# Softmax denominators of two heads in one product, and the extra MLP columns in one matmul per term

## The chip, the core and the metric

The kernel runs on one core of a Trainium2 chip. The metric is the device time of one launch in microseconds (us). Runs of one kernel on this core mostly agree within 0.3%. A run that is over 1.5% above the fastest of its kernel counts as slow and is left out of the ratios. The profile is of one execution; its "span" is some 1.8 us shorter than the device time. The engines are PE (matmul; PEld is its weight load), DVE (vector), ACT (scalar), POOL, and SP, which issues the transfers. The granted clock is the share of full speed at which the profile shows PE running.

## The reference

For four tokens of width 576: a layer norm, then the sum of three things.

```python
def reference(A_x, A_k_cache, A_v_cache, A_wq, A_wo, B_x, B_w1, B_w2, B_w3, B_w4):
    xn = _layernorm(A_x)
    return A_x + _A_ref(xn, ...) + _B_ref(xn, ...)
# _A_ref: 32 query heads on 16 K/V heads of 128, one query per token, softmax over
#         the last 2048 keys of the cache, then @ wo
#     scores = einsum(q, k) * Dh**-0.5;  p = softmax(scores);  o = einsum(p, v);  o @ wo
# _B_ref: a mixer (whose shifted part is zero for one token) and an MLP with 4608 columns
#     x1 + gelu(layernorm(x1) @ w3) @ w4
```

The K and V windows are 67 MB of bf16, the weights wq, wo, w3 and w4 another 20 MB. All of it is read once.

## The kernel before

Each of the 16 K/V heads is loaded as one K tile and one V tile of 2.1 MB, from a pool of six such tiles. The heads pass through a software pipeline with one "turn" per head. In turn t, head t gets its scores, head t-1 its softmax, head t-2 its product with V, head t-3 its output scaling and transposes. The parts that the change touches:

```python
    def sm_exp(h):
        E[h] = ptp.tile([P, SC, QD], BF16, tag="e", name="E", bufs=1)
        rs = small.tile([P, 1], F32, tag="rs", bufs=3)
        nc.scalar.activation(out=E[h][:]..., in_=S_ps.pop(h)[:], func=ACT.Exp, scale=scale, accum_out=rs[:])
        st["rs", h] = rs
    def sm_den(h):       # sums the denominators over the partitions of one query, on PE
        dn = ps_m.tile([P, 1], F32, tag="m", name="dn")
        nc.tensor.matmul(out=dn[:], lhsT=same_j[:], rhs=st.pop(("rs", h))[:], start=True, stop=True)
        st["dn", h] = dn
    def sm_rec(h):
        rd = small.tile([P, 1], F32, tag="rd", bufs=4)
        nc.vector.reciprocal(out=rd[:], in_=st.pop(("dn", h))[:])
        st["rd", h] = rd
    def o_scale(h):
        O_sb[h] = bigp.tile([P, NSL, Dh], F32, tag="big", name="O_sb")
        nc.scalar.activation(out=O_sb[h][:], in_=O_ps.pop(h)[:], func=ACT.Copy, scale=st.pop(("rd", h))[:, 0:1])
    ...
    for t in range(Hkv):
        hm, hv, hf, hp = t - 1, t - 2, t - 3, t - 4
        for s in range(NSL):
            ...
            if s == 0:
                if hm >= 0: sm_max(hm)
                if hv >= 0: sm_rec(hv)
                ...
                if hf >= 0: o_scale(hf)
                k_transpose(t, 1)
```

In turn 7 the MLP's first product (w3) is done in three rounds. In the third, 128 columns that w4 needs in another order are multiplied as three strided matmuls per term; DVE moves the transposed results on:

```python
    if e and r == 2:
        for lo, rhs in x_cols(w3[:, base + m:base + F // 2]):     # 16, 12 and 100 columns, permuted
            ...
            mms.append((row[:, lo:hi, 1].rearrange(...), rhs))
    ...
    nc.vector.tensor_copy(out=xs[0:NX, NFM:, :], in_=gT_all[0:NX, n * m:, 0:B])
    nc.vector.tensor_copy(out=xs[:, NFM - 1, :], in_=gT_ps[:, 0, 1, 0:B])
```

## Time and profile before

| kernel before | value |
|---|---|
| device time, median of 6 runs | 211.56 us (211.21 to 211.69) |
| PE, DVE, ACT busy | 149.7, 114.4, 34.1 us of 209.6 |
| transfer queue, share of 16 DMA engines' span | 97.6% |
| bytes read | 87.17 MB, about 430 GB/s in the steady slices |
| start of PE's last 12 products / end of the span | 205.9 / 209.6 us |

Busy time is a sum over a whole run, so 71% of PE does not say whether PE is ever waited for. The transfers' row of the slices does (the page cuts the span into 40 slices and gives for each the busy share in tenths).

### The profile page before, as it was taken

To read this page: it belongs to the slowest core of one execution; us is meant where nothing else is said; L and a number is where in the kernel's file an instruction comes from. 1 tells how busy PE (TensorE), PEld (TensorE's weight loads), DVE (VectorE), ACT (ScalarE), POOL (GpSimd) and SP (SyncE) were. 2 spreads that over 40 slices of the span, in tenths; PEclk is the share of its full clock that TensorE was granted. 3 is DMA by queue.
4 is the path that set the end of the run, shared out by engine and by line. 5 is a ranking of instruction groups with operands and counts; after the bars stand their busy time and mean duration, and the time that the engine had idled before them with its cause. 6 is when DMAs were issued, how large, how long until landed. Compare 5 with 4: busy or idle time off the path is not lost.

```text
span 209.6 us, 2422 instructions
## 1 busy us (share of the span) xinstructions
PE 149.7 (71%) x984; PEld 60.1 (29%) x998; DVE 114.4 (55%) x167; ACT 34.1 (16%) x64; POOL 9.0 (4%) x32
## 2 busy tenths in 40 slices
PE   0357297599690039668999989659895956898794
PEld 0123132233130013223444333213331312343452
DVE  3611877895910083926507898465949391764100
ACT  7612201021020001111120312110111111113100
POOL 4610000000000000000000300000000000000000
PEclk9999589999787559788999999997998796999679
DMA  7999999999999999999999999999999999999992
GB/s 301 400 419 431 428 435 428 431 427 422 470 401 424 438 425 425 437 435 428 435 431 428 428 415 445 425 438 419 433 441 422 421 439 438 423 424 450 421 399 84
DMA packets 6703, 87.33 MB, mean 417 GB/s; under 512 B 758, under 2 KB 1034, under 8 KB 1700
## 3 DMA queue, kind: packets, MB, share of 16 engines
q1 hardware_dynamic: 6684, 87.17, 97.6%
q8 instruction: 8, 0.13, 0.2%
q10 hardware_dynamic: 8, 0.00, 0.0%
q14 instruction: 3, 0.02, 0.0%
HBM read 87.17 MB, written 0.00 MB: 416 GB/s over the span
## 4 chain that ended last, share of the span: by engine, by line
DMA 66%; DVE 15%; PE 13%; issue 2%; ACT 1%; SPq 1%; POOL 1%; DVEq 0%; POOLq 0%; ACTq 0%
DMA kn<-in_A_k_cache_dram 42%; DVE kt L253 12%; DMA vn<-in_A_v_cache_dram 10%; DMA w_sb<-in_B_w_dram 7%; DMA wq_sb<-in_A_wq_dram 6%; PE S L366 4%; PE g_ps L495 3%; PE q_ps L310 2%; PE oT L431 1%; PE O L418 1%; PE acc L212 1%; DVE PT L400 1%; DVE mx L372 1%; PE S L388 1%; DVE qz L342 1%
## 5 line engine op out<-in xcount | busy, mean ns | idle before, releaser
L366 PE MATMUL S<-kt,qz 128*128 128x512 bf16 x242 | 73.7, 427 | 33.9 <-DVE kt L253 31.9
L253 DVE STREAM_TRANSPOSE kt<-kn 128x2048 int32<-128x2048 int32 x32 | 73.4, 2296 | 26.1 <-DMA kn<-in_A_k_cache_dram 24.7
L366 PEld LDWEIGHTS <-qz 128*128 128x128 bf16 x256 | 23.9, 107 | 62.9 <-issue 45.8
L418 PE MATMUL O<-vn,PT 128*32 128x512 bf16 x256 | 23.4, 406 | 8.0 <-DMA vn<-in_A_v_cache_dram 8.0
L394 ACT ACTIVATE E<-S 128x512 bf16<-128x512 f32 x16 | 9.5, 597 | 96.6 <-PE S L388 96.6
L400 DVE STREAM_TRANSPOSE PT<-E 128x512 bf16<-128x512 bf16 x16 | 11.4, 710 | 13.9 <-ACT E L394 13.9
L425 ACT ACTIVATE O_sb<-O,rd 128x512 f32<-128x512 f32 x16 | 11.0, 687 | 37.2 <-PE O L418 37.2
L441 DVE TENSOR_REDUCE on<-oT 128x8 bf16<-128x128 f32 x16 | 4.6, 290 | 19.8 <-PE oT L431 19.8
L418 PEld LDWEIGHTS <-PT 128*32 128x32 bf16 x256 | 5.8, 94 | 29.4 <-issue 29.1
L431 PE MATMUL oT<-ident_w,O_sb 128*128 128x128 f32 x64 | 12.6, 333 | 0.3 <-ACT O_sb L425 0.3
L372 DVE TENSOR_REDUCE mx<-S 128x1 f32<-128x512 f32 x16 | 10.5, 658 | 1.2 <-PE S L366 1.1
L431 PEld LDWEIGHTS oT<-ident_w,O_sb 128*128 128x128 f32 x64 | 8.2, 164 | 5.3 <-issue 4.3
L388 PE MATMUL S<-nm,j_row 8*128 8x512 bf16 x16 | 6.5, 404 | 1.9 <-DVE nm L384 1.7
L404 PE MATMUL dn<-rs,same_j 128*128 128x1 f32 x32 | 6.2, 264 | 0.4 <-DVE g_x L523 0.4
L404 PEld LDWEIGHTS dn<-rs,same_j 128*128 128x128 f32 x32 | 5.0, 195 | 4.4 <-issue 3.7
L495 PE MATMUL g_ps<-w_sb,ln2T 128*32 128x512 bf16 (+5 forms) x65 | 6.2, 406 | 0.0
L354 PE MATMUL S<-negbig,ohT 4*128 4x512 bf16 x16 | 6.2, 385 | 0.0
L310 PE MATMUL q_ps<-wq_sb,xnT 128*32 128x512 bf16 x40 | 4.2, 610 | 2.1 <-DMA wq_sb<-in_A_wq_dram 2.1
L212 PE MATMUL acc<-wo_sb,op 128*4 128x288 bf16 x64 | 5.5, 324 | 0.0
L212 PE MATMUL acc<-w_sb,gT 128*4 128x288 bf16 x70 | 5.1, 298 | 0.4 <-DMA w_sb<-in_B_w_dram 0.4
L523 DVE COPY g_x<-gT_ps 128x64 f32<-128x64 f32 (+1 forms) x3 | 0.6, 198 | 8.2 <-PE gT_ps L509 8.2
L527 POOL TENSOR_TENSOR g_u<-g_x 128x180 f32<-128x180 f32 x1 | 0.5, 487 | 103.1 <-DVE g_x L523 103.1
(92 smaller groups left out, 79.2 us busy)
## 6 DMA issues: line engine op xcount, KB each, us to landing
kn<-in_A_k_cache_dram SPq DMA_DIRECT2D x16, 2048.0 KB, 25.7
vn<-in_A_v_cache_dram SPq DMA_DIRECT2D x16, 2048.0 KB, 21.7
wo_sb<-in_A_wo_dram SPq DMA_DIRECT2D x4, 1152.0 KB, 37.5
w_sb<-in_B_w_dram SPq DMA_DIRECT2D x1, 4608.0 KB
wq_sb<-in_A_wq_dram SPq DMA_DIRECT2D x1, 4096.0 KB
w_sb<-in_B_w_dram SPq DMA_DIRECT2D x1, 2592.0 KB, 11.0
w_sb<-in_B_w_dram SPq DMA_DIRECT2D x2, 576.0 KB, 34.1
w_sb<-in_B_w_dram SPq DMA_DIRECT2D x1, 864.0 KB
```

Source lines behind the costliest of these rows:

```text
L212: nc.tensor.matmul(out=acc_of(i), lhsT=lhsT, rhs=rhs[:, i * CW:(i + 1) * CW], start=False, stop=False, skip_group_check=True)
L253: nc.vector.transpose(out=kt[:], in_=src)
L366: nc.tensor.matmul(out=S_ps[h][:], lhsT=qz[:, z0:z0 + P], rhs=kt[:, ib, c0:c0 + SC, e:2 * QD:2].rearrange("p c k -> p (c k)"), start=False ...
L372: nc.vector.reduce_max(out=mx[:], in_=S_ps[h][:], axis=AX.X)
L388: nc.tensor.matmul(out=S_ps[h][:], lhsT=j_row[:], rhs=st.pop(("nm", h))[:, 0:1].to_broadcast([NJ, NW]), start=False, stop=False, skip_grou ...
L394: nc.scalar.activation(out=E[h][:].rearrange("p c k -> p (c k)"), in_=S_ps.pop(h)[:], func=ACT.Exp, scale=scale, accum_out=rs[:])
L400: nc.vector.transpose(out=PT[h][:], in_=E.pop(h)[:])
L404: nc.tensor.matmul(out=dn[:], lhsT=same_j[:], rhs=st.pop(("rs", h))[:], start=True, stop=True)
L418: nc.tensor.matmul(out=O_ps[h][g * QD:(g + 1) * QD], lhsT=PT[h][:, c, :], rhs=vn[:, :, c, :], start=(s == 0), stop=False, skip_group_check ...
L425: nc.scalar.activation(out=O_sb[h][:], in_=O_ps.pop(h)[:], func=ACT.Copy, scale=st.pop(("rd", h))[:, 0:1])
L431: nc.tensor.transpose(out=oT[:, s, :], in_=o[:, s, :], identity=ident_w[:, s * NJ:s * NJ + P])
L495: nc.tensor.matmul(out=out, lhsT=ln2T[:, k, :], rhs=rhs, start=(j == 0), stop=False, skip_group_check=True)
```

## The change

It is meant to take instructions off PE and DVE. The row sums of two heads go into two columns of one tile, so one product and one reciprocal serve both. The 128 extra MLP columns are multiplied in their natural order by one matmul per term; ScalarE permutes them while it copies them out, and takes over three DVE copies, now in five pieces. The core of the diff:

```diff
     def sm_exp(h):
-        rs = small.tile([P, 1], F32, tag="rs", bufs=3)
+        if h % 2 == 0:
+            st["rs"] = small.tile([P, 2], F32, tag="rs", name="rs", bufs=3)
-                             accum_out=rs[:])
+                             accum_out=st["rs"][:, h % 2:h % 2 + 1])
     def sm_den(h):
+        if h % 2 == 0:
+            return
-        dn = ps_m.tile([P, 1], F32, tag="m", name="dn")
+        dn = ps_m.tile([P, 2], F32, tag="m", name="dn")
     def sm_rec(h):
+        if h % 2 == 0:
+            return
-        rd = small.tile([P, 1], F32, tag="rd", bufs=4)
+        rd = small.tile([P, 2], F32, tag="rd", bufs=4)
         nc.vector.reciprocal(out=rd[:], ...)
+        for k in range(2):
+            st["rd", h - 1 + k] = rd[:, k:k + 1]
     def mlp_g(r):
-                    for lo, rhs in x_cols(w3[:, base + m:base + F // 2]):
-                        ... mms.append((row[:, lo:hi, 1].rearrange(...), rhs))
+                    mms.append((row[:, :, 1], w3[:, base + m:base + F // 2]))
+        if r == 2:
+            for lo, src in x_cols(g_ps[QD:2 * QD, :, 1]):
+                ... nc.scalar.activation(out=g_x[QD:2 * QD, lo:hi]..., in_=src, func=ACT.Copy)
     def mlp_turn(r):
-            nc.vector.tensor_copy(...)      # three on DVE
+            nc.scalar.activation(...)       # five on ScalarE
```

More of the change, by code (lines that the diff above doesn't have):

```diff
@@ L392, in sm_exp @@
         E[h] = ptp.tile([P, SC, QD], BF16, tag="e", name="E", bufs=1)
-        rs = small.tile([P, 1], F32, tag="rs", bufs=3)
+        if h % 2 == 0:
+            st["rs"] = small.tile([P, 2], F32, tag="rs", name="rs", bufs=3)
         nc.scalar.activation(out=E[h][:].rearrange("p c k -> p (c k)"), in_=S_ps.pop(h)[:], func=ACT.Exp, scale=scale,
-                             accum_out=rs[:])
-        st["rs", h] = rs
+                             accum_out=st["rs"][:, h % 2:h % 2 + 1])
     def sm_turn(h):
@@ L402, in sm_den @@
     def sm_den(h):
-        dn = ps_m.tile([P, 1], F32, tag="m", name="dn")
-        nc.tensor.matmul(out=dn[:], lhsT=same_j[:], rhs=st.pop(("rs", h))[:], start=True, stop=True)
-        st["dn", h] = dn
-    def sm_rec(h):
-        rd = small.tile([P, 1], F32, tag="rd", bufs=4)
-        nc.vector.reciprocal(out=rd[:], in_=st.pop(("dn", h))[:])
-        st["rd", h] = rd
+        if h % 2 == 0:
+            return
+        dn = ps_m.tile([P, 2], F32, tag="m", name="dn")
+        nc.tensor.matmul(out=dn[:], lhsT=same_j[:], rhs=st.pop("rs")[:], start=True, stop=True)
+        st["dn"] = dn
+    def sm_rec(h):
+        if h % 2 == 0:
+            return
+        rd = small.tile([P, 2], F32, tag="rd", bufs=4)
+        nc.vector.reciprocal(out=rd[:], in_=st.pop("dn")[:])
+        for k in range(2):
+            st["rd", h - 1 + k] = rd[:, k:k + 1]
     def pv(h, s):
@@ L424, in o_scale @@
         O_sb[h] = bigp.tile([P, NSL, Dh], F32, tag="big", name="O_sb")
-        nc.scalar.activation(out=O_sb[h][:], in_=O_ps.pop(h)[:], func=ACT.Copy, scale=st.pop(("rd", h))[:, 0:1])
+        nc.scalar.activation(out=O_sb[h][:], in_=O_ps.pop(h)[:], func=ACT.Copy, scale=st.pop(("rd", h)))
     def o_turn(h):
@@ L473 @@
     g_sb = {}
+    g_x = const.tile([P, P], F32, name="g_xt")
     def mlp_g(r):
@@ L487, in mlp_g @@
                 if e and r == 2:
-                    for lo, rhs in x_cols(w3[:, base + m:base + F // 2]):
-                        sizes = rhs.shape[1:]
-                        hi = lo + sizes[0] * sizes[1] * (sizes[2] if len(sizes) > 2 else 1)
-                        names = "x y z"[:2 * len(sizes) - 1]
-                        kw = dict(zip(names.split()[1:], sizes[1:]))
-                        mms.append((row[:, lo:hi, 1].rearrange(f"p ({names}) -> p {names}", **kw), rhs))
+                    mms.append((row[:, :, 1], w3[:, base + m:base + F // 2]))
                 for out, rhs in mms:
@@ L499, in mlp_g @@
         nc.scalar.activation(out=g_sb[r][0:m], in_=g_ps[0:m], func=ACT.Copy)
+        if r == 2:
+            for lo, src in x_cols(g_ps[QD:2 * QD, :, 1]):
+                sizes = src.shape[1:]
+                hi = lo + sizes[0] * sizes[1] * (sizes[2] if len(sizes) > 2 else 1)
+                names = "x y z"[:2 * len(sizes) - 1]
+                kw = dict(zip(names.split()[1:], sizes[1:]))
+                nc.scalar.activation(out=g_x[QD:2 * QD, lo:hi].rearrange(f"p ({names}) -> p {names}", **kw),
+                                     in_=src, func=ACT.Copy)
     def mlp_turn(r):
@@ L515, in mlp_turn @@
             for s in range(XS):
-                off = 4 * s if s < XC else 16 if s == XC else 28 + NX * (s - XA)
-                nc.tensor.transpose(out=gT_all[0:NX, n * m + s, :], in_=gs[e1, off:off + NX, 1],
+                off, k = (4 * s, 4) if s < XC else (16, 12) if s == XC else (28 + NX * (s - XA), NX)
+                nc.tensor.transpose(out=gT_all[0:k, n * m + s, :], in_=g_x[e1, off:off + k],
                                     identity=ident_f[e1, e1])
-            nc.vector.tensor_copy(out=xs[0:NX, NFM:, :], in_=gT_all[0:NX, n * m:, 0:B])
-            nc.vector.tensor_copy(out=xs[:, NFM - 1, :], in_=gT_ps[:, 0, 1, 0:B])
-            dst = xs[:, 16:18, :].unsqueeze(2)
-            gT_ps = gT_ps[:, :, 0:1]
+            for lo, hi, k in ((XB, XC, 4), (XC, XA, 12), (XA, XS, NX)):
+                nc.scalar.activation(out=xs[0:k, NFM + lo:NFM + hi, :],
+                                     in_=gT_all[0:k, n * m + lo:n * m + hi, 0:B], func=ACT.Copy)
+            nc.scalar.activation(out=xs[:, NFM - 1, :], in_=gT_ps[:, 0, 1, 0:B], func=ACT.Copy)
+            nc.scalar.activation(out=xs[:, 16:18, :], in_=gT_ps[:, :, 0, 0:B], func=ACT.Copy)
+            return
         nc.vector.tensor_copy(out=dst, in_=gT_ps[:, :, :, 0:B])
```

## The prediction

> **What bounds the kernel now.** I read the page first (busy shares, the slices, the queues), then the chain of waits, then the queue's own issues against what had been moved, then the last 5 us of the timeline. The page of the kernel before, parts 1 to 4:
>
> ```profile
> PE 149.7 (71%) x984; PEld 60.1 (29%) x998; DVE 114.4 (55%) x167; ACT 34.1 (16%) x64; POOL 9.0 (4%) x32
> ...
> DMA  7999999999999999999999999999999999999992
> GB/s 301 400 419 431 428 435 428 431 427 422 470 401 424 438 425 425 437 435 428 435 431 428 428 415 445 425 438 419 433 441 422 421 439 438 423 424 450 421 399 84
> ...
> q1 hardware_dynamic: 6684, 87.17, 97.6%
> ...
> DMA 66%; DVE 15%; PE 13%; issue 2%; ACT 1%; SPq 1%; POOL 1%; DVEq 0%; POOLq 0%; ACTq 0%
> ```
>
> No compute engine is near full, while the transfer queue works 97.6% of all 16 engines' span; only the first and the last slice are below 9. The GB/s row is flat at about 430 from slice 4 to slice 37. 87.17 MB at 430 GB/s is 203 us of a 209.6 us span.
>
> The chain gives 28% to DVE and PE, which looks like time to be won. It is not: the chain follows what released each issue (a K transpose or a row maximum frees a buffer), but while it passes through DVE or PE the DMA row is still at 9. I added up the bytes issued by the sync engine and took off those moved by the GB/s row. Just before each K or V load the queue still held 5.5 MB or more (12.7 us of work at 430 GB/s) up to 168 us, 3.5 MB (8 us) before the last V load at 179.7, and 1.3 MB (3 us) before the six w4 pieces at 189.7. It never ran dry.
>
> The end, from the timeline of the last 5 us (start, duration, engine, line, operation, idle before):
>
> ```profile
> 204.78 0.78 PE L212 MATMUL acc<-w_sb,gT 128*4 128x288 bf16 x10
> ...
> 205.94 1.04 PE L212 MATMUL acc<-w_sb,gT 128*4 128x288 bf16 x12 [0.39 <-DMA w_sb<-in_B_w_dram]
> ...
> 207.02 0.45 DVE L670 CAST fin<-acc 4x288 bf16<-4x288 f32 x1 [7.47 <-PE acc L212]
> ```
>
> PE has caught up, waits 0.39 us for the last w4 piece, does 12 products, and the result is copied and stored. So the time is: last byte landed (205.9) plus 3.7 us. Only what makes the last byte land earlier, or lets PE be late by over 0.39 us there, can move it.
>
> **What the Trainium skill says.** "DMA: Bandwidth & Descriptors", Measured: a 16 MB load reaches 425 GB/s on a core whose pair is idle, and Where 436 GB/s comes from puts the ceiling of the ports at 435.2. The trace agrees: its steady slices hold 415 to 450, mean about 430. There is nothing left to gain in rate, so the bytes set the time, and the change moves no bytes. "ScalarE: Activation LUTs", What ACT_TABLE_LOAD costs: an ACTIVATE with immediates takes 186 ns + 0.833 ns per element of a partition. The trace: the 128x512 copy (L499) took 597 ns against 612 so worked out, the 64x256 one 377 against 399; close enough to size the new small copies.
>
> **The change part by part.** The rows concerned (line, engine, operation, count, busy us, mean ns), from the groups by form:
>
> ```profile
> L404 PE MATMUL dn<-rs,same_j 128*128 128x1 f32 x32 | 6.2, 264 | 0.4 <-DVE g_x L523 0.4
> L404 PEld LDWEIGHTS dn<-rs,same_j 128*128 128x128 f32 x32 | 5.0, 195 | 4.4 <-issue 3.7 <-ACT E L394 0.7
> L495 PE MATMUL g_ps<-w_sb,ln2T 128*32 128x128 bf16 x5 | 2.0, 406 | 0.0
> L495 PE MATMUL g_ps<-w_sb,ln2T 128*32 128x100 bf16 x5 | 1.6, 330 | 0.0
> L409 DVE RECIPROCAL rd<-dn 128x1 f32<-128x1 f32 x16 | 2.6, 161 | 0.0
> L495 PE MATMUL g_ps<-w_sb,ln2T 128*32 128x16 bf16 x5 | 1.0, 198 | 0.0
> L495 PE MATMUL g_ps<-w_sb,ln2T 128*32 128x12 bf16 x5 | 0.9, 173 | 0.0
> L519 DVE COPY g_x<-gT_ps 20x40 f32<-20x40 f32 x1 | 0.2, 186 | 0.0
> L523 DVE COPY g_x<-gT_ps 128x8 f32<-128x8 f32 x1 | 0.1, 144 | 0.0
> L520 DVE COPY g_x<-gT_ps 128x4 f32<-128x4 f32 x1 | 0.1, 140 | 0.0
> ```
>
> - Denominators: 16 products (each recorded as two matmuls, 32 in all) become 8 of two columns. Gone in records: 16 x 264 ns = 4.2 us of matmul, 16 x 195 ns = 3.1 us of weight load. These overlap; in the timeline the next product starts 0.25 us after the pair's first, so PE wins 8 x 0.25 = 2.0 us.
> - Reciprocals: 8 of 16 go, 8 x 161 ns = 1.3 us of DVE records; the chain counts only 0.07 us each where one lies on it, because the next transpose starts before its record ends. So 0.6 to 1.3 us.
> - MLP round 3: three products per term of 16, 12 and 100 columns become one of 128. PE has 10 products fewer; the 25 of that stretch took 2.43 us, 0.097 each, so 1.0 us.
> - ScalarE gains eight copies: 16, 12 and 100 elements, then 16, 4, 20, 4 and 8. By the formula above 199 + 196 + 269 + 199 + 189 + 203 + 189 + 193 = 1.6 us (estimate), on an engine that is 16% busy. DVE loses three copies, 186 + 140 + 144 ns = 0.5 us.
>
> Sum: PE 3.0 us less, DVE 1.1 to 1.8 us less, ACT 1.6 us more, POOL and DMA unchanged. Beside a transfer queue that is never empty, all of it lies in hidden time: 0 us of it on the path that sets the end.
>
> **What it moves.** The built order shows the pair's reciprocal at the head of each odd head's turn, just behind the row maximum. An even head's output scaling used a reciprocal made one turn earlier; now it waits for this one. Scaling started at 44.80 with a reciprocal at 46.04 to 46.20 in that turn: 1.4 us later; in the MLP turn 97.40 against 99.48: 2.1 us. Its consumer, the output transposes, started at 47.78 in that turn (102.51 in the other): a scaling from 46.25 with its 0.69 us ends at 46.94, 0.8 us ahead. So the late scaling is absorbed, seven times over. Head 14, in the tail: its reciprocal moves from 190.41 to 192.84, its scaling from 192.55 to about 193.05; PE takes its transposes only at 195.85, behind head 15's products, which wait for the last V at 194.67. Absorbed too.
>
> In the MLP turn the five late copies end some 0.2 to 0.6 us after the DVE ones did (114.58), so tanh and the scaling of head 5 behind it on ACT come that much later; PE waited 0.31 us for that scaling already. PE's 1.0 us won just before pays for some of it. The result gT is first used at 192.74.
>
> **Rivals.**
> - *Compute was the bound after all.* For it: 28% of the chain, and turns from 118 to 133 us where DVE works without a pause. If PE's whole 3.0 us came off, 208.6 us. Against: DMA share 1.00 and 428 to 433 GB/s in that very stretch.
> - *A new wait takes its place*: scaling behind the pair's reciprocal, or ACT's copies in the MLP turn, hold PE up. Even 0.5 us in each of eight turns would be 4 us of compute: against it the 0.8 us slack; and it would have to eat 12.7 us of queue first. If it did nonetheless, 212 to 215 us.
> - *The tail*: PE has only 0.39 us in hand before the last w4 piece. Were the last heads to finish 1 us later, the end would come 0.6 us later: 212.2 us. Against it: head 14's slack of over 2 us.
>
> **Range and chances.** The transfers set the time and don't change: 211.5 us. Three runs before lay between 211.21 and 211.69; I allow as much again for another chip and for a little of the second and third rivals: 210.7 to 212.3. A change of 2% is 4.2 us, more than all that PE and DVE win together on the path (so faster is 0.01), and slower by as much needs a dry queue (0.02).
>
> **What would show it.** Right: DMA row at 9 throughout, queue share near 97.6%, last w4 piece landing near 205.9 with a wait of PE on it; PE busy down by some 5 us of records, 16 matmuls of L404 fewer, 10 of the MLP fewer, ACT up by about 1.6 us; even heads' scaling waiting on the reciprocal instead of on the product. Wrong: a slice of the DMA row below 9 in the middle, a transfer wait between issue and an empty queue, or PE with no wait before its last 12 products.

## More of the kernel before

One more view of the kernel before is needed later: what ACT's output scaling waits for. These are rows of ACT's timeline (start us, duration us, engine, line, operation; in brackets the idle time before it and what ended it):

```profile
44.80 0.69 ACT L425 ACTIVATE O_sb<-O,rd 128x512 f32<-128x512 f32 x1 [2.45 <-PE O L418]
52.06 0.69 ACT L425 ACTIVATE O_sb<-O,rd 128x512 f32<-128x512 f32 x1 [2.45 <-PE O L418]
62.40 0.69 ACT L425 ACTIVATE O_sb<-O,rd 128x512 f32<-128x512 f32 x1 [2.45 <-PE O L418]
```

Every one of them starts when the product with V is done; the reciprocal is there already.

## The result, and the profile after

| | before | after |
|---|---|---|
| device time, median of 6 runs | 211.56 us | 211.38 us |
| lowest, highest | 211.21, 211.69 | 211.25, 211.52 |
| ratio after/before | | 0.9994 (0.9981 to 1.0007) |
| span of the profiled run | 209.6 us | 209.6 us |

A ratio here is the mean time of one kernel's fast runs over the mean of the other's in the same rounds, so it is not quite the ratio of the medians. The change has no measurable effect.

The page of the changed kernel, in the same order as the lines that the prediction shows of before:

```profile
PE 150.2 (72%) x958; PEld 58.2 (28%) x972; DVE 113.4 (54%) x156; ACT 34.8 (17%) x72; POOL 9.0 (4%) x32
...
DMA  7999999999999999999999999999999999999992
...
q1 hardware_dynamic: 6684, 87.17, 97.7%
...
DMA 66%; DVE 15%; PE 14%; ACT 1%; issue 1%; SPq 1%; DVEq 0%; ACTq 0%
```

The transfers' row is the same to the digit, the queue's share is 97.7% against 97.6%. PE has 26 matmuls fewer (984 to 958), yet its busy time rose by 0.5 us. That is the clock: the mean granted clock of this run was 0.868 against 0.885, and the score products that the change does not touch took 437 ns each instead of 427 (464 at 0.816 in the profile of run 7, 400 at 0.969 in that of run 9). PE's busy time is no measure of a change of this size; the count is.

The groups that the change touched, by form (line, engine, operation, count, busy us, mean ns, then idle before):

```profile
L406 PE MATMUL dn<-rs,same_j 128*128 128x2 f32 x16 | 3.5, 287 | 0.0
L413 DVE RECIPROCAL rd<-dn 128x2 f32<-128x2 f32 x8 | 1.3, 163 | 0.0
L507 ACT ACTIVATE g_xt<-g_ps 32x100 f32<-32x100 f32 x1 | 0.2, 233 | 0.0
L529 ACT ACTIVATE g_x<-gT_ps 20x20 f32<-20x20 f32 x1 | 0.2, 159 | 0.0
```

Two columns cost little more than one did (287 and 163 ns against 264 and 161), so nearly half of that work is gone. ACT's eight copies took 146 to 233 ns each, 1.3 us in all; its busy time rose by only 0.7 us because they overlap.

The output scaling on ACT, for the same three heads as shown of before:

```profile
46.19 0.69 ACT L430 ACTIVATE O_sb<-O,rd 128x512 f32<-128x512 f32 x1 [3.94 <-DVE rd L413]
51.71 0.69 ACT L430 ACTIVATE O_sb<-O,rd 128x512 f32<-128x512 f32 x1 [2.16 <-PE O L423]
77.63 0.69 ACT L430 ACTIVATE O_sb<-O,rd 128x512 f32<-128x512 f32 x1 [17.49 <-DVE rd L413]
```

Even heads (first and third row) now wait for the pair's reciprocal. The first is 1.4 us late, as worked out. The third is 15 us late, which was not worked out: in that turn the reciprocal stands on DVE behind a row maximum that waits for a K tile still being transferred. PE pays neither: over the whole run its output transposes waited 0.3 us for the scaling, before and after.

The end of the span:

```profile
205.92 1.01 PE L212 MATMUL acc<-w_sb,gT 128*4 128x288 bf16 x12 [0.61 <-DMA w_sb<-in_B_w_dram]
...
206.64 0.29 PE L212 MATMUL acc<-w_sb,gT 128*4 128x288 bf16 x2
...
206.96 0.45 DVE L681 CAST fin<-acc 4x288 bf16<-4x288 f32 x1 [8.11 <-PE acc L212]
```

PE's last visible wait ends at 205.92 us, before it was 205.94. PE comes to it earlier by 0.2 us and waits 0.61 instead of 0.39 us. (The second row is a part of the first: the last two of the 12 products. They start at 206.64; run 12 shows why that matters.) Further up, after the MLP turn, the changed kernel issues its K loads about 1 us earlier (116.81 against 117.76, 131.31 against 132.36). By 167.94 (167.99 before) nothing is left of it: the next K and V come when the queue delivers them.

### The profile page after: what moved, and what is told of

Same layout as the page of the kernel before. It is cut to its first block, busy times and chain, and to the rows that moved or that the text cites. A ratio compares the mean times of both kernels' runs of the same rounds, so it can differ in the third digit from the quotient of the medians.

```text
span 209.6 us, 2356 instructions
## 1 busy us (share of the span) xinstructions
PE 150.2 (72%) x958; PEld 58.2 (28%) x972; DVE 113.4 (54%) x156; ACT 34.8 (17%) x72; POOL 9.0 (4%) x32
## 3 DMA queue, kind: packets, MB, share of 16 engines
q1 hardware_dynamic: 6684, 87.17, 97.7%
## 4 chain that ended last, share of the span: by engine, by line
DMA 66%; DVE 15%; PE 14%; ACT 1%; issue 1%; SPq 1%; DVEq 0%; ACTq 0%
DMA kn<-in_A_k_cache_dram 43%; DVE kt L253 12%; DMA vn<-in_A_v_cache_dram 10%; DMA w_sb<-in_B_w_dram 7%; DMA wq_sb<-in_A_wq_dram 6%; PE S L366 5%; PE g_ps L496 2%; PE q_ps L310 2%; PE O L423 1%; PE oT L436 1%; DVE PT L400 1%; PE acc L212 1%; DVE mx L372 1%; PE S L388 1%; ACT E L395 1%
## 5 line engine op out<-in xcount | busy, mean ns | idle before, releaser
L366 PE MATMUL S<-kt,qz 128*128 128x512 bf16 x242 | 76.4, 437 | 32.2 <-DVE kt L253 30.4
L423 PE MATMUL O<-vn,PT 128*32 128x512 bf16 x256 | 23.9, 414 | 9.3 <-DMA vn<-in_A_v_cache_dram 9.3
L496 PE MATMUL g_ps<-w_sb,ln2T 128*32 128x512 bf16 (+2 forms) x55 | 5.5, 441 | 0.0
L212 PEld LDWEIGHTS <-gT 128*4 128x4 bf16 (+3 forms) x90 | 4.2, 89 | 3.1 <-issue 1.0
```

What stands on the lines that cost most here:

```text
L212: nc.tensor.matmul(out=acc_of(i), lhsT=lhsT, rhs=rhs[:, i * CW:(i + 1) * CW], start=False, stop=False, skip_group_check=True)
L366: nc.tensor.matmul(out=S_ps[h][:], lhsT=qz[:, z0:z0 + P], rhs=kt[:, ib, c0:c0 + SC, e:2 * QD:2].rearrange("p c k -> p (c k)"), start=False ...
L423: nc.tensor.matmul(out=O_ps[h][g * QD:(g + 1) * QD], lhsT=PT[h][:, c, :], rhs=vn[:, :, c, :], start=(s == 0), stop=False, skip_group_check ...
L496: nc.tensor.matmul(out=out, lhsT=ln2T[:, k, :], rhs=rhs, start=(j == 0), stop=False, skip_group_check=True)
```

## The experiments

The theory: the bytes set the end, and the change's saving is real but hidden. The rivals: compute sets the end and two effects of opposite sign cancel; or the late scaling and ScalarE's copies give back what PE and DVE save; or the tail decides. Times are medians; each ratio is to the kernel before in the same rounds. All twelve kernels' outputs were within the tolerance, even where values were made wrong; so the check does not see such errors here (that the attention's part of the output is small would explain it, and was not measured).

**1 and 2. Each part alone.** The first takes the new `sm_exp`, `sm_den` and `sm_rec` with the MLP of before, the second the reverse.

```diff
 e1_den_only: changed kernel with
-    mlp_g, mlp_turn of the change
+    mlp_g, mlp_turn of before
 e2_mlp_only: kernel before with
-    mlp_g, mlp_turn of before
+    mlp_g, mlp_turn of the change
```

> The denominators and reciprocals in pairs, the MLP as before. Theory (transfers set the end): 211.2 to 211.7 us, the ratio within 0.3% of 1. Rival (two effects of opposite sign cancel: the late scaling costs 8 x 0.5 us or the fewer products win 2 us, the MLP part the reverse): at least 1 us away from 211.5, in the opposite direction to the MLP part alone.

> The MLP part alone, the denominators as before. Theory (transfers set the end): 211.2 to 211.7 us. Rival (cancelling effects): at least 1 us away from 211.5, in the opposite direction to the denominators alone.

Measured: 211.57 us, ratio 1.0005 (0.9992 to 1.0017), and 211.58 us, ratio 1.0006 (0.9992 to 1.0019). Neither part does anything, so there is no pair of effects of 1 us that cancel.

**3. One K load less.**

```diff
-        nc.sync.dma_start(out=t[:]..., in_=win[:, h]...)
+        if kind == "K" and h == 9:
+            nc.gpsimd.memset(t[:]..., 0.0)
+        else:
+            nc.sync.dma_start(out=t[:]..., in_=win[:, h]...)
```

> The changed kernel with one K load of 2.1 MB (head 9) replaced by zeros written by the idle POOL: a wrong result on purpose, all compute instructions stay. Theory (transfers set the end, 430 GB/s): 4.9 us less, 206.5 us (206.0 to 207.0). Rival (DVE and PE on the chain set the end, the transfers are hidden): under 2 us less, 209.5 to 211.5 us.

Measured: 206.61 us, ratio 0.9772 (0.9756 to 0.9789), that is 4.8 us less. The whole transfer time of the tile (2.097 MB at 430 GB/s are 4.9 us) comes off the end, although every compute instruction is still there. This is the strongest evidence for the theory: it takes away transfer time and no work of an engine.

**4. Ten microseconds more for DVE.**

```diff
-        nc.vector.reduce_max(out=mx[:], in_=S_ps[h][:], axis=AX.X)
+        for _ in range(2):
+            nc.vector.reduce_max(out=mx[:], in_=S_ps[h][:], axis=AX.X)
```

> The changed kernel with the row maximum done twice in each turn: 16 x 0.65 us = 10 us more DVE work, several times what the change takes off DVE and PE. Theory (transfers set the end and the queue holds 8 to 12 us of work): 211.2 to 211.9 us. Rival (the chain's DVE and PE shares set the end): half or more of the 10 us appears, 216 us or more.

Measured: 211.47 us, ratio 1.0003 (0.9990 to 1.0017). The page of this run:

```profile
PE 149.5 (71%) x972; PEld 57.3 (27%) x972; DVE 124.2 (59%) x172; ACT 34.9 (17%) x72; POOL 9.0 (4%) x32
...
DMA  7999999999999999999999999999999999999992
...
q1 hardware_dynamic: 6684, 87.17, 97.8%
```

DVE is busy for 124.2 us instead of 113.4, and the time has not moved. Adding the issued bytes and taking off the moved ones, as the prediction did, leaves at least 5.3 MB (12 us) queued before each K or V load up to 168 us. If 10 us more cost nothing, the 1 to 2 us that the change takes off DVE cannot gain anything.

**7. Thirty microseconds more.** The same edit with the maximum done four times.

> The changed kernel with the row maximum done four times in each turn: 16 x 1.95 us = 31 us more DVE work. A turn bound by DVE becomes 7.25 + 1.95 = 9.2 us, near the 9.8 us that its K and V take to transfer. The theory expects most of it hidden still, 212 to 218 us, with the transfer row below 9 in some slices and K or V issued later; the rival (DVE on the path) expects 235 us or more.

Measured: 222.05 us, ratio 1.0471 (1.0433 to 1.0508), 10 us more; the profiled run, slow, is used for the pattern alone. The expected 212 to 218 was missed. The reason is seen in the transfers' row of that run:

```profile
DMA  7989999999999999999999999999999999998000
GB/s 283 464 385 435 418 437 432 432 429 453 426 401 443 432 416 445 432 429 429 426 435 432 423 432 433 432 429 429 429 419 445 429 427 431 426 415 344 2 0 1
```

The transfers are all but full to the end (slice 3 is at 8), and end in slice 37 of 40 in a span of 223.1 us, that is before 207 us, nearly as early as in the full kernels. The expectation that the row would be below 9 in the middle failed; instead compute fell so far behind that some 16 us of it were left when the last piece had landed (207.1), where the kernels of before and after have some 3. So the slack is finite: over 10 us and under 31 us of DVE work, spread over the turns.

**5 and 6. Half of K and V gone, filled by POOL: a faulty instrument.** The same edit as in 3 for 16 loads, in the kernel before and in the changed one.

> The kernel before with 16 of the 32 K and V loads (33.5 MB) replaced by zeros that POOL writes: wrong result on purpose, compute instructions unchanged. 53.6 MB at 430 GB/s are 125 us, so compute should bind: 16 turns of 7.25 us as in the stretch from 122.8 to 130.0, a start of 22.5 us and an end of some 12 us make about 150 us (140 to 165). It is the base for the next run.

> The changed kernel with the same 16 loads replaced by zeros. With the transfers out of the way, the theory (the change does save compute, hidden in the full kernel) expects 0.7 to 2.5 us less than the kernel before with the same loads gone: the MLP part some 1 us, the halved reciprocals 0.6. The rival (the late scaling and ScalarE's copies give it back) expects no difference within 0.3 us, or more time.

Measured: 203.59 us (195.01 to 205.77, all but one run counted slow) and 202.07 us. The expected 150 us is missed by far, the two can't be compared, and the cause is in the experiment itself. A timeline of the first (a slow run, used for the pattern alone):

```profile
112.64 3.51 POOL L104 MEMSET kn<- 128x4096 f32 x1
...
114.17 5.45 DVE L377 TENSOR_SCALAR dm<-sel_g,mx 128x16 bf16<-128x16 bf16 x1
114.31 5.32 DVE L412 RECIPROCAL rd<-dn 128x1 f32<-128x1 f32 x1
114.39 5.24 DVE L256 STREAM_TRANSPOSE kt<-kn 128x2048 int32<-128x2048 int32 x1
116.09 3.51 POOL L104 MEMSET vn<- 128x4096 f32 x1
```

The tiny `dm` on DVE, 0.23 us elsewhere, lasts 5.45 us, and ends at 119.62, when POOL's memsets end (119.60). The Trainium skill, "SBUF — State Buffer", Who interferes with whom, has this: VectorE and GpSimd share a port pair, a `tensor_scalar` can run in the mode that needs it, and whoever comes second blocks until the first has finished. The trace agrees. How much it cost is seen in the chain that ended last: the `dm` has 16% of it, some 32 us of 203.0, against 1% in run 8, whose span without POOL's memsets is 170.6. A filler that is meant to be free must not use POOL here. (Run 3 had one such memset; no `dm` is stretched in its trace.)

**8 to 11. No V loads at all, and POOL left alone.** The V products read one small tile of zeros, so PE does as many as before; 33.5 MB are not loaded. PE ran at a granted clock of 0.96 to 0.98 in these runs, against 0.87 to 0.90 in the kernels before and after, so they show where the saving is, not what the full kernel would win. The count of free K and V tiles follows (not shown).

```diff
-        vn = kv_tiles["V", h][:].rearrange("p (s c) d -> p s c d", s=NSL)
-            nc.tensor.matmul(out=O_ps[h]..., lhsT=PT[h][:, c, :], rhs=vn[:, :, c, :], ...)
+            nc.tensor.matmul(out=O_ps[h]..., lhsT=PT[h][:, c, :], rhs=vzero[:], ...)
-NKV = 6
+NKV = 5
```

> The kernel before with all 16 V loads (33.5 MB) gone: the V products read one small tile of zeros instead, five K buffers instead of six to make room, nothing extra on POOL. Wrong result on purpose. 53.6 MB at 430 GB/s are 125 us, so compute should bind: 16 turns of 7.25 us (the pace from 122.8 to 130.0 in the full kernel), a start of 22.5 and an end of 12 us make 150 us (140 to 160), with the transfer row well below 9 in later slices. Base for the next three.

> The changed kernel with all V loads gone in the same way. Theory (the change saves compute, which the transfers hide in the full kernel): 0.7 to 2.5 us less than the kernel before without V loads; DVE sets the turns, so 8 x 0.08 us of reciprocals, 1 us of the MLP products, and little from the 2 us of PE. Rival (the late scaling and ScalarE's copies give it back): within 0.3 us or slower.

> The pairs of denominators alone, without V loads. Theory: 0.3 to 1.3 us less than the kernel before without V loads (8 reciprocals off DVE at 0.08 to 0.16 us each). Rival (the late scaling costs): 0 or more.

> The MLP part alone, without V loads. Theory: 0.5 to 1.5 us less than the kernel before without V loads (10 products fewer at 0.097 us, three DVE copies fewer), once, in turn 7. Rival (ScalarE's copies delay what follows): 0 or more.

| without V loads | median | ratio to the full kernel before (95%) |
|---|---|---|
| before | 171.81 us | 0.8112 (0.8083 to 0.8141) |
| after | 169.28 us | 0.7997 (0.7974 to 0.8020) |
| denominators alone | 170.60 us | 0.8043 (0.8017 to 0.8069) |
| MLP part alone | 170.27 us | 0.8032 (0.8009 to 0.8054) |

With the transfers out of the way the change is worth 0.8112 - 0.7997 = 0.0115 of 211.5 us, 2.4 us; the two intervals do not touch. At an equal clock it is less: three runs of before at 0.97 took 170.5 to 171.3 us and three of the changed kernel 169.2 to 169.4, which is 1.6 us between the means. So the saving is real and is not given back. The 171.8 us missed the expected 150 (140 to 160): the pace of 7.25 us a turn came true, but I had left out that the MLP turn takes 16 us and the turns with an output projection over 8. The transfers' row of the kernel before without V loads:

```profile
DMA  6999999999999999999999996800696799000000
...
PE 35%; DVE 30%; DMA 26%; issue 3%; ACT 3%; POOL 1%; SPq 0%; ACTq 0%; DVEq 0%; POOLq 0%
```

The zeros at the right are what a compute bound looks like here. Where the gain lies is read from the start of the row maximum of each turn, a beat of the pipeline. These are the ones on either side of the MLP turn, first the kernel before, then the changed one, both without V loads:

```profile
77.54 0.65 DVE L374 TENSOR_REDUCE mx<-S 128x1 f32<-128x512 f32 x1
93.52 0.67 DVE L374 TENSOR_REDUCE mx<-S 128x1 f32<-128x512 f32 x1
```

```profile
77.41 0.65 DVE L374 TENSOR_REDUCE mx<-S 128x1 f32<-128x512 f32 x1
92.37 0.65 DVE L374 TENSOR_REDUCE mx<-S 128x1 f32<-128x512 f32 x1
```

The MLP turn takes 15.98 us before and 14.96 after: 1.02 us less. It is 14.95 with the MLP part alone and 15.86 with the denominators alone, so the MLP part gives it. In the changed kernel with all loads, the 15 products of that stretch are one row of the timeline:

```profile
108.19 1.79 PE L496 MATMUL g_ps<-w_sb,ln2T 128*32 128x256 bf16 x15
```

The 25 of before took 2.43 us, so the products give 0.64 us, and the same 2.43 and 1.79 stand in the runs without V loads. The other 0.4 us come in front of the row maximum: before, it starts at 93.52 behind the three small DVE copies (from 93.26), which are now ScalarE's.

From the second of these row maxima to the last it is 59.05 us before, 58.63 after, 58.80 with the denominators alone, but 59.48 with the MLP part alone, whose denominators are those of before. So the pairs give some 0.3 to 0.4 us over eight turns, and that is no more than this stretch varies. Together it is about 1.4 us, near the 1.6 at an equal clock.

The rest of the 2.4 us goes with the clock: in the profiled run of before, the 70 closing products took 5.85 us against 4.45 in the other three; runs of before at 0.96 took 172.4 us, and only one of five of the changed kernel was at 0.96. Whether fewer PE instructions bring the better clock, or chance did, these runs do not tell. The parts by the ratios (1.5 and 1.7 us) exceed the whole; their ratios leave out three runs of 171.6 to 172.1 us as slow, while the 172.4 of before count as fast. By the medians of all runs the parts are 1.2 and 1.5 us and the whole 2.5.

**12. The tail.** The prediction took the end for "last byte plus 3.7 us". PE seemed to do the 12 products of the last three w4 pieces in one go, so merging them looked free.

```diff
-    W4_PIECES = [0, NFH, NFM - 11, NFM - 6, NFM - 2, NFM - 1, NFM]
+    W4_PIECES = [0, NFH, NFM - 11, NFM - 6, NFM]
```

> The changed kernel with the last three w4 pieces (4, 1 and 1 rows of 1152 bytes per partition) as one transfer. PE does the 12 products of these three in one go after its last wait anyway, so the merge loses no overlap and has fewer short packets. If the end is the last byte plus a fixed 3.7 us, the time moves only with that byte: 211.0 to 211.5 us, at most 0.4 us faster. If instead the small last pieces let PE start earlier, it is 0.3 us or more slower.

Measured: 212.08 us, ratio 1.0034 (1.0021 to 1.0048): 0.7 us slower, which is the second branch of the expectation, and the only edit here that moved the time without touching bytes or adding much work. PE in that run:

```profile
206.49 0.90 PE L212 MATMUL acc<-w_sb,gT 128*4 128x288 bf16 x12 [1.28 <-DMA w_sb<-in_B_w_dram]
```

The span is 0.6 us longer (210.2 against 209.6). The last step of the transfers in the chain that ended last (start and duration from issue to landing), first of the changed kernel, then of this one:

```profile
191.35 14.53 DMA w_sb<-in_B_w_dram
```

```profile
191.26 15.19 DMA w_sb<-in_B_w_dram
```

In the changed kernel the load issued at 191.35 is the piece of 576 KB, not the last: it lands at 205.88 and frees PE at 205.92. By the trace's semaphore events the two pieces of 144 KB land at 206.24 and 206.60, while PE works on its first eight products, and the last two products start at 206.64, right behind the last piece (the row shown above). The kernel before has the same order: 205.90, 206.30 and 206.66. The merged piece lands at 206.45, 0.15 us earlier than the last small one, but then all 12 products (0.90 us) are still to be done, and the result is copied at 207.42 instead of 206.96. So the bytes do not come later; what is lost is the work that PE did while they came. No version with all its loads was faster than both kernels.

## Why the prediction was right

- **The bound.** "0 us of it on the path that sets the end": held, 211.38 against 211.5 forecast. Run 3 shows that bytes count one for one, run 4 that 10 us of compute do not. "Steady slices hold 415 to 450" was read too narrowly (the row has 401 and 470 too); the mean of about 430 stands.
- **The queue's slack.** "It never ran dry": held for the changed kernel too (at least 14 us queued before each K or V load up to 168 us, from the same sum). Runs 4 and 7 put it between 10 and 31 us of extra DVE work. The bytes still queued were the right sign, not the full measure: compute may also lag behind the landed data until the end.
- **The savings.** MLP 1.0 us: the 1.02 measured where it can be seen agrees by luck. The ten products gave 0.64 us, not 1.0, since a mean over 25 was taken for the narrow ones that went; the DVE copies in front of the row maximum made up the rest. Denominators: the count halved as said, but the 2.0 us of PE are not seen in any time, and even without V loads they gave 0.3 to 0.4 us, less than the 0.6 to 1.3 put down for DVE alone.
- **The busy times.** "PE busy down by some 5 us of records" failed: it rose by 0.5 us, the clock being lower. ACT's 1.6 us was 1.3 by the sum of the records and 0.7 in busy time.
- **The late scaling.** 1.4 us late as said in one turn, 2.4 against "2.1" in the MLP turn, but 15 us in a third. "Seven times over" was said from two turns worked out, and the third was not among them. The conclusion held: PE's transposes waited 0.3 us for it before and after.
- **The MLP turn's tail.** "0.2 to 0.6 us later" failed in sign: the last copy was issued at 113.21 and the tanh began at 115.09 instead of 116.34, since what went before it outweighed ACT's copies: the products took 0.64 us less, and no denominator product stands in that turn of the changed kernel.
- **The tail.** PE's wait before the last 12 products is there (0.61 us), so the rival of a late tail is out. "PE waits for the last w4 piece" and "last byte landed (205.9) plus 3.7 us" were misread: at 205.9 the third last piece had landed, the last one at 206.66 before and 206.60 after, and the end is some 3 us behind that. The forecast did not suffer, because the change touches none of this; run 12, built on the misreading, did.

## What to carry to other kernels

Before pricing instructions, ask whether the transfer queue is ever empty and what PE waits for last (a merged row of the timeline can hide a later wait); if the answer is "never" and "a load", a saving on the engines is worth nothing now, however large its share of the chain. Test it in both directions: take away a load and see the whole of it come off, add compute and see nothing happen. A filler that stands in for a load is an instruction too, and must be checked for what it blocks.

## What the Trainium skill lacked or had wrong

- "ScalarE: Activation LUTs", What ACT_TABLE_LOAD costs: 186 ns plus 0.833 ns per element is some 25 to 45 ns too much for small copies out of PSUM. 4 elements took 146 ns (189 worked out), 20 took 159 (203), 100 took 233 (269; its row is shown above).
- "Perfetto Trace Analysis", Per-engine timelines, says that DVE runs strictly in order and that a record begins when execution begins. When POOL held DVE up, three DVE records in a row started 0.14 and 0.08 us apart and lasted 5.2 to 5.5 us each, so such a start does not mean that work was going on.
- No page says what cutting the last transfer of a full queue is worth: with the last 864 KB in pieces of 576, 144 and 144 KB, PE began on them at 205.92 us and the result was copied 0.46 us earlier than with one piece, which landed at 206.45.
